# Top-32 attention with a squared-ReLU feed-forward: the end of the kernel rearranged

## The chip, the core and the metric

The kernel runs on one core of a Trainium2 chip. It is one program, launched once. The time is the device time of that launch in microseconds, the median of several runs. TensorE (PE) multiplies matrices, VectorE (DVE), ScalarE (ACT) and GpSimd (POOL) work elementwise, and SyncE (SP) issues nearly all DMAs. Each engine takes its instructions strictly in the order in which they were written down; semaphores tie the engines together.

## The reference

```python
B, H, S, D = 8, 8, 576, 64
scores = matmul(q, k.T) / sqrt(D)                      # (B, H, S, S)
kth    = 32nd largest of each row of scores
scores = where(scores >= kth, scores, -1e9)
attn   = exp(scores - max); attn = attn / (sum(attn) + 1e-9)
x = (attn @ v).transpose(0, 2, 1, 3).reshape(B*S, H*D) # (4608, 512)
h = x @ w_in                                           # (4608, 2048)
r = maximum(h, 0); g = r * r
out = g @ w_out                                        # (4608, 512), float32
```

Inputs and the output are float32. The attention scores are made in float32, attention weights times values and the feed-forward part in bfloat16.

## The kernel before

The attention rows are cut into 144 groups, numbered 0 to 143. A group is two blocks of 128 query rows (one for each of two heads) against all 576 keys. Each group goes through the same steps:

1. **Scores.** TensorE writes them into three PSUM banks (`ps<-qk`, L449). ScalarE copies them to one of six `s` buffers (`s<-ps`, L622).
2. **Top 32.** VectorE first takes the maximum of pairs and fours of columns (`ps<-ps,s` and `m<-ps,s` on L678, `f<-m,ps` on L688); POOL forms the other members of the pairs with integer sums and differences (L673). Then VectorE alternates "eight largest" (`c<-f`, L705) and "replace them" (`f<-c,f`, L709) three times, and a last "eight largest" over all 576 columns gives the 32nd value (`kth<-f`, L712). The cheap path assumes that the largest values are spread in a certain way over the columns.
3. **Flip.** ScalarE makes a penalty from `s` and `kth` (`w<-s,kth`, L720). TensorE transposes `s` and adds the steep penalty on top (`ps<-ident,s` on L452 and `ps<-steep_bf,w` on L449, nine blocks of 128 columns; the ninth uses the bank that the maxima of another group use). ScalarE takes the exponential (`p<-ps`, L754).
4. **Values.** TensorE multiplies with the values (`ps<-vb,p`, L449), ScalarE copies (`av<-ps`, L781), VectorE takes the reciprocal of the row sums (`rzall<-av`, L783), POOL scales (`x<-av,rzall`, L785), TensorE transposes (`ps<-ident_bf,x`, L452), ScalarE copies into a chunk of `xt` (L809).

When a chunk of rows has all its heads, it goes through the feed-forward part, in the function `feed`: TensorE multiplies with `win` (`ps<-xt,win`, L449), ScalarE takes the ReLU (`g<-ps`, L835), some engine squares it (`g<-g`; POOL on L849, ScalarE on L852, VectorE on L846), TensorE multiplies with `wo` (`ps<-wo,g`, L449), ScalarE copies the result (`o<-ps`, L869) and SP stores it (L877). The last two chunks have 128 rows each: 64 products `xt,win`, four squares of 128x512, and 16 products `wo,g` each. These products, the transposes of `x` and the value products share the two banks of the PSUM pool `psum`.

**Who sets the order.** Nothing is ordered by hand. Each step is declared with an engine, an assumed duration, a priority (a due time, smaller first), the tiles that it reads, writes and takes, and sometimes an extra delay. A list scheduler (`Plan.schedule`) then plays the program through on these assumed durations, and on each engine the ready step with the smallest priority goes next. The order that results is written out for each engine, with semaphore waits where needed. The constants shift due times: `TL` draws the attention steps after `kth` of the last 32 groups forward, `LAGL` delays the feed-forward steps of the chunks of the last batch (not the very last chunk), `LATE` delays the reciprocals, `SQ` chooses which squares go to POOL, `WC` is the due time of the weight casts. A change of a constant can so move instructions far from the place that it is about.

**The verdict.** The cheap top-32 is exact only for rows that meet its assumption. `verdict` checks this for all rows at once: VectorE compares the collected values and reduces them and `rzall` to three numbers per partition in `fone` (L978 to L986), TensorE sums them over the partitions with a product of one column (`ps<-fone`, L988), VectorE reduces the three sums to the integer `flag` (L990). Its steps have the priority 1e6, so they go last on their engines. Then every engine loads `flag` into a register and branches (L1022 to L1024): if it is above zero, the whole attention is done again with an exact program, `again`; with the inputs here it is zero and the branch skips that program. SP first waits until all stores of the main program have landed.

Of the kernel before, what the change touches and what calls it, by code (L numbers as in the profile page):

```python
# [291 lines left out]
def bass_top_k_attn__then__act_relu_squared_kernel(  # L292
# [31 lines left out]
    MQ = 19.61  # L324
    MP = 18.0
    MA = 18.27
    SQ = 5.15
    TA = 7.2
    TW = -0.14
    TL = 18.33  # L330
    WARM = 8
    WP = 6.49
    BW = 1
# [1 line left out]
    WEND = 70  # L335
    NL = 31.89
    WD = 3.33
    WC = 1.75
    WA = 1.13
    WN = 6  # L340
    NBO = 3.81
    LAG = 12.93
    STEP = 2.98
    LATE = 2.07
    LAGL = 17.86

    ident32 = sb("ident32", [P, P])
    ident_bf = sb("ident_bf", [P, P], BF16)
# [10 lines left out]
    fone = sb("fone", [P, 4])  # L359
# [31 lines left out]
    def tile(nm):  # L391
        return Tile(pools[nm])
# [4 lines left out]
    def bank(t, i=0):  # L397
        return ps32[:, BASE[t.pool.name] + t.slot + i, :]
# [8 lines left out]
    em = Emitter(nc)  # L407
    act, vec, gp, pe = nc.scalar, nc.vector, nc.gpsimd, nc.tensor
# [23 lines left out]
    CHUNKS = [[(0, 0, 128)], [(0, 128, 128)], [(0, 256, 256)]] if B0Q else [[(0, 0, 256)], [(0, 256, 256)]]  # L432
# [15 lines left out]
    def mm(o, l, r, start, stop=True):  # L448
        return pe.matmul(o, l, r, start=start, stop=stop, skip_group_check=True)  # L449
# [6 lines left out]
    def build(full, weights, pl):  # L456
# [358 lines left out]
        def feed(chunk, xt, tm, step):  # L815

            nt = sum(n_ for _, _, n_ in chunk)
            b = chunk[-1][0]
            last, end = b == NB - 1, chunk is CHUNKS[-1]
            kf = max(1, 512 // nt)  # L820
            lag = 0 if end else LAGL if last else LAG
            gs = [tile("g") for _ in range(NFB // kf)]
            for i, g in enumerate(gs):
                hh = Tile(psum)

                def fh(hh=hh, i=i):
                    for f in range(kf):
                        fb = kf * i + f
                        for ct in range(NCT):
                            ins = mm(bank(hh)[:, nt * f:nt * f + nt], win[:, ct, 128 * fb:128 * fb + 128],  # L830
                                     at(xt)[:, ct, 0:nt], ct == 0 and f == 0)
                    return ins

                def fr(hh=hh, g=g):
                    return act.activation(at(g)[:, 0:kf * nt], bank(hh)[:, 0:kf * nt], ACTF.Relu)  # L835

                tf = tm + step * i
                w_ = kf * nt
                ho = pl.op("pe", .03 + kf * 4 * (nt / 2340 + .002), tf + lag, fh, r=[xt], w=[hh], take=[hh, g],
                           after=weights if chunk not in FIRST else weights and weights[NCT * (kf * i // 8):][:NCT],  # L840
                           nbf=tf if not last else 0)
                if chunk in FIRST and weights:
                    first_h.append(ho)
                pl.op("act", .19 + w_ / 1200, tf + lag + .5, fr, r=[hh], w=[g])
                if end:
                    pl.op("dve", .1 + w_ / 1900, tf + lag + .8, lambda g=g: vec.tensor_tensor(  # L846
                        at(g)[:, 0:w_], at(g)[:, 0:w_], at(g)[:, 0:w_], ALU.mult), u=[g])
                elif last or i * SQ % 8 < SQ:
                    pl.op("gp", .15 + w_ / 480, tf + lag + 1, lambda g=g: gp.tensor_tensor(  # L849
                        at(g)[:, 0:w_], at(g)[:, 0:w_], at(g)[:, 0:w_], ALU.mult), u=[g])  # L850
                else:
                    pl.op("act", .19 + w_ / 1200, tf + lag + 1, lambda g=g: act.activation(  # L852
                        at(g)[:, 0:w_], at(g)[:, 0:w_], ACTF.Square), u=[g])
            for tb in range((nt + 127) // 128):
                n_ = min(128, nt - 128 * tb)
                op_, ob = Tile(psum), tile("o")
                to = tm + step * (len(gs) + 1 + 4 * tb)
                for sub in range(4):
                    def fo(sub=sub, op_=op_, tb=tb, n_=n_):
                        for fb in range(4 * sub, 4 * sub + 4):  # L860
                            c = nt * (fb % kf) + 128 * tb
                            ins = mm(bank(op_)[0:n_, :], at(gs[fb // kf])[:, c:c + n_], wo[:, fb, :], fb == 0)
                        return ins

                    pl.op("pe", .9, to + lag + step * sub, fo,
                          r=sorted({gs[fb // kf] for fb in range(4 * sub, 4 * sub + 4)}, key=lambda t: t.num),
                          w=[op_], take=[op_, ob] if sub == 0 else [], after=weights[8 + 2 * sub:10 + 2 * sub], order=[ho],
                          nbf=to + step * sub if not last else 0)
                pl.op("act", .6, to + lag + 4 * step, lambda op_=op_, ob=ob, n_=n_: act.copy(  # L869
                    at(ob)[0:n_, :], bank(op_)[0:n_, :]), r=[op_], w=[ob])  # L870
                rows, at_ = [], 0
                for b_, r0, m_ in chunk:
                    lo_, hi_ = max(at_, 128 * tb), min(at_ + m_, 128 * tb + n_)
                    if lo_ < hi_:
                        rows.append((lo_ - 128 * tb, hi_ - lo_, S * b_ + r0 + lo_ - at_))
                    at_ += m_
                pl.op("sp", 2.3, to + lag + 4 * step + 1, lambda ob=ob, rows=rows: [nc.sync.dma_start(  # L877
                    out[row:row + m_, :], at(ob)[p0:p0 + m_, :]) for p0, m_, row in rows],
                    r=[ob], ndma=len(rows), sem=lambda o: f"o{o.tiles[0].slot}")
# [13 lines left out]
        for b in range(NB):  # L893
# [3 lines left out]
            for hp, gi in seq:  # L897
# [6 lines left out]
                if state.get("more"):  # L904
                    state.pop("more")()
                tt = tg + PER + 2 - TA - TL * max(0, 1 - (NGRP - state["n"]) / NL)
                pt = attend(gi, st, wt, tt)
# [65 lines left out]
    def verdict(pl, kths, rzs):  # L973

        t = Tile(psum)
        G = NGRP
        fc = fcmp[:, :].rearrange("p (l g) -> p l g", l=2)
        x = pl.op("dve", .4, 1e6, lambda: vec.tensor_tensor(fc, c16[:, :, 0:G], c24[:, :, 0:G], ALU.min), after=kths)  # L978
        x = pl.op("dve", .4, 1e6, lambda: vec.tensor_tensor(fc, c8[:, :, 0:G], fc, ALU.min), after=[x])
        done = [pl.op("dve", .4, 1e6, lambda: vec.tensor_tensor(fc, kth[:, :, 0:G], fc, ALU.is_gt), after=[x])]  # L980
        d = pl.op("dve", .35, 1e6, lambda: vec.tensor_reduce(fone[:, 0:1], fcmp[:, :], AX.X, ALU.max), after=done)
        e = pl.op("dve", .35, 1e6, lambda: vec.tensor_reduce(fone[:, 1:2], rzall[:, :], AX.X, ALU.max), after=rzs)
        f = pl.op("dve", .35, 1e6, lambda: vec.tensor_reduce(fone[:, 2:3], rzall[:, :], AX.X, ALU.min), after=rzs)
        e = pl.op("dve", .1, 1e6, lambda: vec.tensor_scalar(
            fone[:, 1:2], fone[:, 1:2], 1e30, None, ALU.is_gt), after=[e])
        f = pl.op("dve", .1, 1e6, lambda: vec.tensor_scalar(  # L986
            fone[:, 2:3], fone[:, 2:3], 1e-30, None, ALU.is_lt), after=[f])
        g = pl.op("pe", .1, 1e6, lambda: pe.matmul(bank(t)[0:1, 0:3], fone[:, 3:4], fone[:, 0:3],  # L988
                                                   start=True, stop=True), w=[t], take=[t], after=[d, e, f])
        return pl.op("dve", .1, 1e6, lambda: vec.tensor_reduce(flag[:, :], bank(t)[0:1, 0:3], AX.X, ALU.max), r=[t])  # L990

    main = Plan()
# [19 lines left out]
    def stored(pl):  # L1012
        return {o.idx[0]: o.idx[1] for o in pl.order["sp"] if o.idx[0][1].startswith("o")}

    with nc.Block() as blk:
        def emit(e, eng):
            em.via(main, e)
            em.emit(main, e, eng)
            if e == "sp":
                for kk, vv in stored(main).items():  # L1020
                    eng.wait_ge(em.sem(kk), vv)
            eng.wait_ge(em.sems["dve"], flagged.idx[1])  # L1022
            val = eng.value_load(flag[0:1, 0:1], min_val=0, max_val=P)
            with eng.If(val > 0):  # L1024
                em.emit(again, e, eng)
                if e == "sp":
                    for kk, vv in stored(again).items():
                        eng.wait_ge(em.sem(kk), vv)

        @blk.gpsimd  # L1030
        def _(g_):
            emit("gp", g_)

        @blk.tensor
        def _(pe_):
            emit("pe", pe_)

        @blk.vector
        def _(v_):
            emit("dve", v_)  # L1040

        @blk.scalar
        def _(a_):
            emit("act", a_)

        @blk.sync
        def _(s_):
            emit("sp", s_)
# [28 lines left out]
```

## Time and profile before

| | |
|---|---|
| five runs | 869.27, 869.32, 870.0, 870.72, 875.24 us; median 870.0 |
| profiled execution | 869.82 us, its span 867.9 us, 22690 instructions |
| mean granted TensorE clock | 0.997 |
| last `kth` of VectorE (group 143) ends | 836.55 us |
| last product with `wo` on TensorE ends | 860.58 us |
| busy VectorE, TensorE, POOL, ScalarE | 824.1, 828.1, 788.1, 759.9 us |

The span runs from the first to the last instruction of the profiled execution; its own time is 1.9 us longer. Busy time counts computing instructions. Waits, loads of registers and branches are not counted; they appear under the line numbers of their source with the name of the engine's sequencer (SPq, PEldq and so on). L449 and L452 are helpers through which nearly all matrix products go, so these are told apart by their tiles.

### The profile page before, as it was taken

The numbers are of one execution on the slowest core, as the hardware profiler recorded it, in microseconds if no ns is written. First come the engines' busy times: TensorE is split into PE (matmuls) and PEld (weight loads), VectorE is DVE, ScalarE is ACT, GpSimd is POOL, SyncE is SP. The second block draws the span as 40 slices with busy tenths as digits, with TensorE's granted clock in tenths as the row PEclk, the third lists the DMA queues.
The fourth block names the chain that finished last, engine by engine and source line by source line (L and its number), as shares of the span: only waits on it lengthen the run. The fifth ranks groups of instructions, "written<-read, shape, count | busy, mean of one in ns | idle before, by whom it ended". The sixth has DMA issues, their size and how long they took to land.

```text
span 867.9 us, 22690 instructions
## 1 busy us (share of the span) xinstructions
PE 828.1 (95%) x8057; PEld 609.8 (70%) x8057; DVE 824.1 (95%) x3414; ACT 759.9 (88%) x1261; POOL 788.1 (91%) x826
## 2 busy tenths in 40 slices
PE   8898899999999999999999999999999999999996
PEld 3565677667776777767778677777778667687774
DVE  3899999999999999999999999999999999999970
ACT  3788999889998899989999799998989889898872
POOL 6798999999999989999999989999999988998961
PEclk9999999999999999999999999999999999999998
DMA  7583422111310223012120121301231021000001
GB/s 177 119 200 103 126 47 63 28 41 34 91 43 14 59 65 76 22 35 61 35 77 16 39 68 44 96 14 41 57 82 29 14 53 30 26 2 14 26 14 41
DMA packets 126985, 48.21 MB, mean 56 GB/s; under 512 B 119184, under 2 KB 119184, under 8 KB 126864
## 3 DMA queue, kind: packets, MB, share of 16 engines
q1 hardware_dynamic: 126192, 46.52, 21.4%
q8 instruction: 65, 1.06, 0.5%
q14 instruction: 56, 0.46, 0.2%
q10 hardware_dynamic: 672, 0.16, 0.1%
HBM read 37.22 MB, written 9.44 MB: 54 GB/s over the span
## 4 chain that ended last, share of the span: by engine, by line
DVE 70%; PE 17%; ACT 6%; issue 5%; POOL 1%; DVEq 0%; POOLq 0%
DVE f L709 22%; DVE c L705 18%; DVE kth L712 14%; PE ps L449 13%; DVE ps L678 5%; DVE f L688 5%; DVE m L678 5%; PE ps L452 4%; ACT p L754 2%; ACT s L622 1%; ACT w L720 1%; DVE rzall L783 1%; ACT g L835 1%; POOL f L673 0%; POOL t L673 0%
## 5 line engine op out<-in xcount | busy, mean ns | idle before, releaser
L709 DVE MATCH_REPLACE8 f<-c,f 128x104 f32<-128x104 f32 (+2 forms) x864 | 266.7, 314 | 0.0
L705 DVE MAX8 c<-f 128x8 f32<-128x104 f32 (+2 forms) x864 | 243.3, 318 | 0.1
L720 ACT ACTIVATE w<-s,kth 128x576 bf16<-128x576 f32 x288 | 223.2, 785 | 22.6 <-DVE kth L712 21.6
L452 PE MATMUL ps<-ident,s 128*128 128x128 f32 x1296 | 222.0, 280 | 9.2 <-ACT p L754 5.6
L673 POOL TENSOR_TENSOR t<-s 128x576 int32<-128x576 int32 x144 | 202.6, 1412 | 20.0 <-ACT s L622 19.9
L449 PE MATMUL ps<-qk 64*128 64x64 f32 (+3 forms) x1280 | 207.0, 442 | 2.9 <-DVE m L678 2.3
L712 DVE MAX8 kth<-f 128x8 f32<-128x576 f32 x288 | 207.9, 746 | 0.0
L673 POOL TENSOR_TENSOR f<-t,m 128x576 int32<-128x576 int32 x144 | 203.2, 1411 | 0.0
L449 PEld LDWEIGHTS ps<-qk 64*128 64x128 f32 (+1 forms) x1280 | 128.1, 176 | 77.4 <-issue 60.3
L622 ACT COPY s<-ps 128x1152 f32<-128x1152 f32 x144 | 161.3, 1120 | 22.8 <-PE ps L449 22.4
L754 ACT ACTIVATE p<-ps 128x1152 bf16<-128x1152 f32 x144 | 163.3, 1134 | 13.6 <-PE ps L449 12.6
L452 PEld LDWEIGHTS ps<-ident,s 128*128 128x128 f32 x1296 | 143.1, 141 | 34.2 <-ACT p L754 11.0
L449 PE MATMUL ps<-steep_bf,w 128*128 128x128 bf16 x1296 | 139.9, 219 | 0.0
L449 PE MATMUL ps<-wo,g 128*128 128x512 bf16 x576 | 139.7, 379 | 0.0
L673 POOL TENSOR_TENSOR t<-m 128x288 int32<-128x288 int32 x144 | 114.9, 798 | 18.8 <-ACT m L686 14.3
L449 PE MATMUL ps<-xt,win 128*128 128x256 bf16 (+1 forms) x1152 | 127.0, 261 | 4.1 <-ACT xt L809 2.3
L673 POOL TENSOR_TENSOR f<-t,f 128x288 int32<-128x288 int32 x144 | 114.9, 798 | 0.1
L449 PEld LDWEIGHTS ps<-xt,win 128*128 128x128 bf16 x1152 | 97.3, 98 | 19.7 <-ACT xt L809 3.7
L449 PEld LDWEIGHTS ps<-steep_bf,w 128*128 128x128 bf16 x1296 | 105.1, 100 | 4.0
L849 POOL TENSOR_TENSOR g<-g 128x512 bf16<-128x512 bf16 x92 | 95.5, 1042 | 7.6 <-ACT g L835 7.1
L835 ACT ACTIVATE g<-ps 128x512 bf16<-128x512 f32 x144 | 85.7, 606 | 5.7 <-PE ps L449 4.4
L449 PEld LDWEIGHTS ps<-wo,g 128*128 128x128 bf16 x576 | 51.8, 98 | 48.5 <-ACT g L835 0.5
(67 smaller groups left out, 909.9 us busy)
## 6 DMA issues: line engine op xcount, KB each, us to landing
rv<-in_v_dram SPq DMA_DIRECT2D x64, 128.0 KB, 2.4
out_dram<-o SPq DMA_DIRECT2D x32, 256.0 KB, 2.1
rk<-in_k_dram SPq DMA_DIRECT2D x63, 128.0 KB, 2.5
rq<-in_q_dram SPq DMA_DIRECT2D x62, 128.0 KB, 2.6
g<-in_moe_w_in_dram SPq DMA_DIRECT2D x8, 512.0 KB, 4.1
g<-in_moe_w_out_dram SPq DMA_DIRECT2D x8, 512.0 KB, 4.0
rv<-in_v_dram SPq DMA_DIRECT2D x96, 16.0 KB, 2.2
rq<-in_q_dram SPq DMA_DIRECT2D x32, 32.0 KB, 2.6
```

What stands on the lines that cost most here:

```text
L449: return pe.matmul(o, l, r, start=start, stop=stop, skip_group_check=True)
L452: return pe.matmul(o, i, ident, is_transpose=True, skip_group_check=True, **kw)
L622: cp = [pl.op("act", 1.2, tg - LEAD + 1, lambda: act.copy(at(st)[:, :, :], two(banks(ss), SECOND, S)), r=[ss], w=[st])]
L673: return pl.op("gp", dur, prio, lambda: gp.tensor_tensor(o().bitcast(I32), x().bitcast(I32), y().bitcast(I32), op), **kw)
L678: return vec.tensor_tensor(o, two(banks(ss)[:, a:], SECOND + HALF, QUART), two(at(st)[:, 0, HALF + a:], HALF, QUART), ALU.max)
L705: lambda i=i, t=t, c0=c0, c1=c1: vec.max(eighth(t, i), at(f)[:, i, c0:c1]),
L709: lambda i=i, t=t, c0=c0, c1=c1: vec.match_replace(at(f)[:, i, c0:c1], eighth(t, i), at(f)[:, i, c0:c1], NEG), hold=[f])]
L712: ks.append(chain(kth, i, prev[i] + [low], .665, lambda i=i: vec.max(eighth(kth, i), at(f)[:, i, :]), hold=[f]))
L720: pl.op("act", .77, tw + .8 * i, lambda i=i: act.activation(at(wt)[:, i, :], at(st)[:, i, :], ACTF.Relu, bias=kth[:, i, n:n + 1], scale=-1.0),
L754: pl.op("act", 1.15, tt + 1, lambda: act.activation(at(pt)[:, :, :].rearrange("p k q -> p (k q)"), banks(e)[:, 0:2 * S], ACTF.Exp, scale=0 ...
L835: return act.activation(at(g)[:, 0:kf * nt], bank(hh)[:, 0:kf * nt], ACTF.Relu)
L849: pl.op("gp", .15 + w_ / 480, tf + lag + 1, lambda g=g: gp.tensor_tensor(at(g)[:, 0:w_], at(g)[:, 0:w_], at(g)[:, 0:w_], ALU.mult), u=[g])
```

## The change

Three things are rewritten, and five constants have other values.

- SP reads the flag and branches like the other engines, without a wait before it. It waits for the stores of the main program after the branch, and, where the flag is above zero, inside the branch before it runs `again`.
- The product of the verdict (`ps<-fone`) has the priority 0 instead of 1e6.
- The squares of the last two chunks go to VectorE, not only those of the last one.

```diff
-    SQ = 5.15
+    SQ = 5.21
...
-    TL = 18.33
+    TL = 15.79
...
-    WC = 1.75
+    WC = 2.54
...
-    LATE = 2.07
+    LATE = 2.1
-    LAGL = 17.86
+    LAGL = 15.27
...
+            direct = chunk in CHUNKS[-2:]
...
-                if end:
+                if direct:
                     pl.op("dve", .1 + w_ / 1900, tf + lag + .8, lambda g=g: vec.tensor_tensor(
                         at(g)[:, 0:w_], at(g)[:, 0:w_], at(g)[:, 0:w_], ALU.mult), u=[g])
...
-        g = pl.op("pe", .1, 1e6, lambda: pe.matmul(bank(t)[0:1, 0:3], fone[:, 3:4], fone[:, 0:3],
+        g = pl.op("pe", .1, 0, lambda: pe.matmul(bank(t)[0:1, 0:3], fone[:, 3:4], fone[:, 0:3],
                                                    start=True, stop=True), w=[t], take=[t], after=[d, e, f])
...
             em.emit(main, e, eng)
-            if e == "sp":
-                for kk, vv in stored(main).items():
-                    eng.wait_ge(em.sem(kk), vv)
             eng.wait_ge(em.sems["dve"], flagged.idx[1])
             val = eng.value_load(flag[0:1, 0:1], min_val=0, max_val=P)
             with eng.If(val > 0):
+                if e == "sp":
+                    for kk, vv in stored(main).items():
+                        eng.wait_ge(em.sem(kk), vv)
                 em.emit(again, e, eng)
                 if e == "sp":
                     for kk, vv in stored(again).items():
                         eng.wait_ge(em.sem(kk), vv)
+            if e == "sp":
+                for kk, vv in stored(main).items():
+                    eng.wait_ge(em.sem(kk), vv)
```

## The prediction

> **What bounds the kernel now.** I read the page first (engine shares, chain that ended last), then busy time by stretches, then the timeline from the last top-k group to the end, then the instructions of the verdict's lines.
>
> ```profile
> PE 828.1 (95%) x8057; PEld 609.8 (70%) x8057; DVE 824.1 (95%) x3414; ACT 759.9 (88%) x1261; POOL 788.1 (91%) x826
> DVE 70%; PE 17%; ACT 6%; issue 5%; POOL 1%; DVEq 0%; POOLq 0%
> ...
> 100.00:650.00 550.00, 533.96 (x5231) 399.95 (x5227) 549.81 (x2288) 506.88 (x838) 526.29 (x531) 1.00 0.21 51
> 650.00:740.00 90.00, 88.37 (x883) 66.20 (x884) 89.92 (x376) 82.25 (x140) 82.44 (x84) 1.00 0.13 32
> 740.00:780.00 40.00, 39.93 (x413) 30.20 (x413) 39.92 (x167) 36.50 (x63) 37.89 (x41) 1.00 0.04 15
> 780.00:820.00 40.00, 39.28 (x398) 29.13 (x394) 40.00 (x170) 33.67 (x59) 37.08 (x41) 1.00 0.07 21
> 820.00:836.60 16.60, 16.09 (x212) 13.31 (x210) 16.57 (x71) 14.81 (x27) 13.85 (x17) 1.00 0.05 18
> 836.60:860.60 24.00, 22.62 (x260) 16.32 (x258) 5.64 (x15) 11.33 (x22) 7.90 (x10) 1.00 0.06 23
> 860.60:867.90 7.30, 0.10 (x2) 0.00 (x0) 0.15 (x1) 0.58 (x1) 0.00 (x0) 0.66 0.14 48
> ```
>
> The columns after the length are busy PE, PEld, DVE, ACT, POOL. From 100 to 836.6 us VectorE has no free time (0.4 us of 736.6). TensorE is nearly as full: from 650 to 860.6 it is idle for 1.63+0.07+0.72+0.51+1.38 = 4.3 us. So the kernel has three parts: VectorE's top-k until 836.6, TensorE's feed-forward remainder until 860.6, and 7.3 us in which hardly anything is computed.
>
> ```profile
> 848.14 12.46 PE ps L449 x128
> 860.59 0.02 issue
> 860.62 0.58 ACT o L869
> ...
> L1022 SPq EVENT_SEMAPHORE  x1: 1885/1885/1885, 861.6 to 861.6; - x1
> ...
> L1023 SPq TENSOR_LOAD <-flag x1: 468/468/468, 863.5 to 863.5; - x1
> L1023 SPq FUSED_REGOPS  x1: 183/183/183, 864.0 to 864.0; - x1
> ...
> L1024 ACTq COMPARE_BRANCH  x1: 58/58/58, 861.7 to 861.7; - x1
> L1024 PEldq COMPARE_BRANCH  x1: 4285/4285/4285, 861.8 to 861.8; - x1
> L1024 SPq COMPARE_BRANCH  x1: 45/45/45, 864.4 to 864.4; - x1
> ...
> L1015 PEldq DRAIN  x1: 73/73/73, 866.1 to 866.1; - x1
> L1015 SPq DRAIN  x1: 53/53/53, 867.7 to 867.7; - x1
> ```
>
> The end reads as a chain on SP: last store issued at about 861.2, a wait of 1.885 us for its landing, the load of the flag, register work, a branch at 864.4, and only 3.3 us later the drain with which every engine signs off. The others branched at 861.7 to 861.8 and drained by 866.1. SP is last by 1.5 us.
>
> **SP's branch ahead of the stores.** The wait for the last store moves behind load, register work and branch. SP's load then follows the last store's issue (861.6 instead of 863.5), so the branch comes at 862.4 and the drain, 3.3 us behind it, at 865.7. The store landed at about 863.5, inside those 3.3 us, so the moved wait costs nothing. Queued behind it is only SP's drain, for which all engines wait at the end. Gain 1.9 us. Two limits: PE drains at 866.1, but it waits for the flag today (load at 860.9, once the reduce on VectorE has ended); with the flag earlier its load follows its last matmul at about 860.4, so its drain comes near 865.6, just ahead of SP. If PE does not move, 1.5 us of gain remain. And SP's branch now falls among the others'; if it takes PE's 4.3 us from branch to drain instead of 3.3, 0.9 us remain. I take 1.9, since the three engines that branched together took 3.0 to 3.3.
>
> Advanced Engine Details and Errata (Control Flow Timing) of the Trainium skill gives about 108 ns for a compare-and-branch; SP's 45 ns row is below that, PE's 4285 ns far above. By that figure alone, as an estimate, overlapping the branch would bring 0.1 us plus load and register work, about 0.8 us in all; the rows with the 3.3 us behind the branch say 1.9. Runtime: NRT & Kernel Launch (Instruction fetch mechanics) of the Trainium skill says that a taken branch out of the fetched window stalls on a fetch, which is the kind of gap that these rows have.
>
> **The verdict's product earlier.** One product (two rows of 0.17 us on PE, issued together) and a 0.15 us reduce. Before, they stood behind PE's last matmul (860.51) and beside the 0.58 us copy of the last output, so off the path. Now the product stands in front of four `wo` products of the next-to-last chunk. It needs both reductions of `rzall` (0.45 and 0.44), which follow the last reciprocal: by the walk below 851.4 at the latest against 852 for PE, so no wait is expected; if it misses, PE waits under 1 us. It also takes one of the two banks of `psum` until the reduce, under the 0.86 us of those four products. Cost 0.1 us, bounds 0 and 1.
>
> **Squares of the next-to-last chunk.** Four POOL instructions of 1.04 us go, four VectorE ones come (L846: 577 ns once, 425 three times). VectorE is busy for 5.64 of the last 24.0 us, so the 1.7 to 2.3 us fit. In before the POOL squares ended at 851.96 and their `wo` products started at 853.51, with 64 `xt,win` products in between to hide them. In the new order these `wo` products follow the chunk's own `xt,win` directly, so the square is on PE's path, and 0.43 instead of 1.04 is what makes that order possible: worth nothing by itself.
>
> The 577 ns row is a square that began at 851.66 while POOL squared until 851.96: +0.15 us beside POOL. SBUF — State Buffer (SBUF: two separate sides) of the Trainium skill speaks against the move: a VectorE operation with two SBUF inputs and a GpSimd one that reads SBUF lock each other out for a whole instruction. By it, each of the four squares could wait for a POOL multiply (L785, 0.39): up to 1.6 us; by the row 0.6 us at most, mostly between matmuls.
>
> **The constants.** SQ 5.15 to 5.21 gives the same set of indices for `i*SQ % 8 < SQ`, and with WC 1.75 to 2.54 the start stays as it was: in the order of instructions TensorE, ScalarE, POOL and SP are equal in both kernels for the first half (PE's first difference is at about group 75 of 144), and VectorE differs by single swaps with a reciprocal. So the starved start (VectorE's waits of 3.1 us and less before 66 us) stays. From there the order shifts, at first to and fro, and from group 126 on with one sign, through TL and LAGL: up to the flip of group 135 TensorE has 10.2 us more feed-forward work in front of the same flip (80 `xt,win` of 0.056, 20 `wo` of 0.216, rest scores), up to the last one 3.5 us (16 `wo`). That work is only moved. VectorE's sum is unchanged, so its end stays at 836.6 unless it starves.
>
> What it does to TensorE's end I walk from the last scores. In before they end at 820.24; from there to 860.58 are 40.3 us, 1.9 of them idle (0.16+0.36+0.75+0.63), so 38.4 of work. In the new order 48 `xt,win` (2.7), 8 `wo` (1.7) and one flip block (0.2) stand ahead of the last scores instead: 33.8 us remain. But the last scores now stand behind a flip block that waits for VectorE's `f<-m,ps` of group 142: group 140 ends at 821.64, then in the new order two `c` (0.33), `f` (0.25), `ps` and `m` (0.72), a reciprocal (0.07), `f` (0.25), `f<-m,ps` (0.36): 823.6; plus 0.35 for the block and 1.3 for the scores: 825.3. End: 825.3 + 33.8 + idle. With 0.6 (one bank wait) to 1.9 (as before) it is 859.7 to 861.0; middle 860.4 against 860.58. Bounds: no idle at all since 650 us, -4.3; on the other side the rival below.
>
> **Sum.** Against the profiled execution, 869.82 us (span 867.9 and 1.9 around it; the median of the runs is 870.0, 0.2 higher): -1.9 (SP) -0.2 (TensorE) +0.1 (verdict) = 867.8.
>
> **Rivals.**
> *The order wins back TensorE's idle time* (0.19). The 4.3 us go in part: 2.3 or more gone gives 865.4 and less, all gone 863.5. For: the feed-forward work comes earlier, and the waits in front of the last flips (0.36, 0.75) are between instructions that change places. Against: TensorE still waits for reciprocals, which stand behind 2.4 us of verdict work on VectorE in both orders, now four instead of three.
> *Late flips starve VectorE* (0.14, of it 0.09 over 0.5%). There are six `s` buffers: the scores of group n+6 need the flip of n. In before, by the timeline, the flip ends 5 to 14.5 us after its `kth` (most at group 129), and VectorE has no wait. With the extra work in front it is 17 to 18 us for groups 127 to 136 (129: 14.5+3.5; 132: 10.8+7.0; 135: 7.0+10.2), 3 us beyond anything seen. The new order takes the pair maxima later, at about 4 groups (22.7 us) behind `kth` n; flip, scores (1.3) and copy (1.1) need some 20.5, so 2 us are left. It decides from a lateness of 4 us: 2 of cover and the 1.9 won. With 4 us of starvation 871.8, with 7 us 874.8, all of the 10.2 about 878.
> *The end does not shrink* (0.12): the wait was not the limit, because PE's branch (4.3 us) or a fetch beside the others sets the end. Then 0 to 0.9 is won: 868.8 to 869.7.
> *My forecast* (0.55): 866.2 to 868.8.
>
> **How the numbers follow.** About 0.5% (4.35 us) is what a measurement of this kernel tells from no change. Faster than 865.65 is most of the first rival and a little of the forecast's edge: 0.2. Slower than 874.35: 0.09. The rest 0.71. The range leaves out the deep ends of the first two rivals: 864.0 to 871.0.
>
> **What would show it.** Right: SP's flag load directly behind the last store's issue, its wait for the stores gone or some 17 ns, its drain 4.4 us after that load; other engines' flag loads before 860.9; VectorE's last `kth` within 1 us of 836.6; L449's last `wo` between 859 and 862; eight squares on VectorE of 0.43 to 0.58. Wrong: VectorE waits for `s` copies (`ps` from ACT) after 720 us, a `kth` end beyond 839, or a branch-to-drain gap on SP over 4 us.

## The result and the profile after

The changed kernel takes 867.32 us (median of 38 runs) against 869.23 us for the kernel before (66 runs beside it): ratio 0.9974, interval 0.9967 to 0.9982. That is 1.9 us, or 0.26%: clear of no change with this many runs, though less than the 0.5% that the prediction took as telling. Now and then an execution of either kernel loses some 6 us in its first 100 us (4 of those 66, and some in the groups below, whose intervals they widen); the first profiled execution of the changed kernel was one (873.16 us), so the lines below come from another execution of the same kernel (866.93 us, span 865.1).

In the changed file the load of the flag is L1021 (before L1023), the branch L1022, SP's wait for the stores L1032, the drain L1016, the verdict's product and its reduce L989 and L991, VectorE's squares L847, the ReLU L836, the last copy L870.

The page of the changed kernel, engine shares and the chain that ended last:

```profile
PE 823.2 (95%) x7994; PEld 608.6 (70%) x8057; DVE 825.3 (95%) x3418; ACT 761.7 (88%) x1261; POOL 783.6 (91%) x822
...
DVE 67%; PE 19%; ACT 6%; issue 5%; POOL 2%; DVEq 0%; POOLq 0%
```

VectorE has four instructions more, POOL four fewer: the moved squares. The record lost 63 products (7994 of 8057), so TensorE's busy time is too low here, and its waits are read from the view of waits instead. Busy time by stretches, cut at the end of the last `kth` (836.95) and of the last `wo` product (860.13):

```profile
100.00:650.00 550.00, 530.11 (x5181) 399.44 (x5223) 549.78 (x2286) 506.21 (x838) 526.24 (x532) 1.00 0.21 51
650.00:740.00 90.00, 87.77 (x881) 65.95 (x885) 90.00 (x377) 83.59 (x141) 81.29 (x82) 1.00 0.13 34
740.00:780.00 40.00, 39.22 (x382) 28.57 (x384) 39.41 (x166) 35.71 (x60) 37.24 (x40) 1.00 0.04 15
...
836.95:860.15 23.20, 22.35 (x245) 15.75 (x245) 7.03 (x21) 11.66 (x23) 2.07 (x5) 1.00 0.07 26
860.15:865.10 4.95, 0.00 (x0) 0.00 (x0) 0.00 (x0) 0.58 (x1) 0.00 (x0) 0.78 0.19 63
```

Three differences. The stretch after the last product is 4.95 us instead of 7.3. The one between the last `kth` and the last product is 23.2 instead of 24.0. And VectorE, full before, now lacks 0.59 us between 740 and 780, where it lacked 0.08. The view of waits gives most of that, for VectorE from 100 to 836 us (the same view of before has no line):

```profile
DVE ps L678 <- ACT s L622: 0.3, 1, 0.3
DVE ps L678 <- ACT p L754: 0.2, 1, 0.2
```

These are pair maxima that wait for a new `s` and for the PSUM bank that the exponential frees: VectorE starves by half a microsecond. The same two waits stand in all nine traces with the new constants and in none of the five with the old ones. Late flips explain them: the longer wait ends at 779.74 with the pair maxima of group 135, and the flip of group 129, whose `s` buffer that group takes, had ended only at 777.25, 18.3 us behind its `kth`; the scores of group 135 (to 778.5) and their copy (778.6 to 779.7) filled the 2.5 us between. The end, from the lines of the flag load, branch, SP's wait and drain (first and last start in us):

```profile
L1021 PEldq TENSOR_LOAD <-flag x1: 489/489/489, 857.8 to 857.8; - x1
L1021 SPq TENSOR_LOAD <-flag x1: 501/501/501, 861.2 to 861.2; - x1
...
L1022 PEldq COMPARE_BRANCH  x1: 3912/3912/3912, 858.7 to 858.7; - x1
L1022 SPq COMPARE_BRANCH  x1: 50/50/50, 862.0 to 862.0; - x1
...
L1032 SPq EVENT_SEMAPHORE  x1: 17/17/17, 864.6 to 864.6; - x1
...
L1016 PEldq DRAIN  x1: 73/73/73, 862.7 to 862.7; - x1
L1016 ACTq DRAIN  x1: 80/80/80, 864.4 to 864.4; - x1
L1016 SPq COMPARE_BRANCH  x1: 43/43/43, 864.7 to 864.7; - x1
L1016 SPq DRAIN  x1: 13/13/13, 864.9 to 864.9; - x1
```

SP issues the last store at 860.8, loads the flag at 861.2, branches at 862.0, and needs 2.6 us until its next instruction; the wait there takes 17 ns. SP's drain still comes last, now only 0.5 us behind ScalarE's. PE loads the flag at 857.8, 2.3 us before its last product ends.

### The profile page after: what moved, and what is told of

It is laid out like the page before. It is cut to its first block, busy times and chain, and to the rows that moved or that the text cites. A ratio compares the mean times of both kernels' runs of the same rounds, so it can differ in the third digit from the quotient of the medians.

```text
span 871.3 us, 22671 instructions
## 1 busy us (share of the span) xinstructions
PE 833.8 (96%) x8057; PEld 610.7 (70%) x8057; DVE 825.2 (95%) x3418; ACT 762.3 (87%) x1261; POOL 783.8 (90%) x822
## 4 chain that ended last, share of the span: by engine, by line
DVE 67%; PE 19%; ACT 6%; issue 5%; POOL 1%; DVEq 0%; POOLq 0%
DVE f L709 21%; DVE c L705 17%; PE ps L449 15%; DVE kth L712 14%; DVE ps L678 5%; DVE f L688 5%; DVE m L678 5%; PE ps L452 5%; ACT p L754 2%; ACT s L622 1%; ACT w L720 1%; ACT g L836 1%; DVE rzall L783 1%; POOL t L673 0%; ACT qk L579 0%
## 5 line engine op out<-in xcount | busy, mean ns | idle before, releaser
L449 PE MATMUL ps<-qk 64*128 64x64 f32 (+3 forms) x1280 | 209.3, 445 | 2.7 <-DVE m L678 2.1
L449 PEld LDWEIGHTS ps<-xt,win 128*128 128x128 bf16 x1152 | 96.9, 98 | 18.4 <-ACT xt L809 2.7
L850 POOL TENSOR_TENSOR g<-g 128x512 bf16<-128x512 bf16 x88 | 91.6, 1044 | 4.9 <-ACT g L836 3.8
L836 ACT ACTIVATE g<-ps 128x512 bf16<-128x512 f32 x144 | 86.2, 606 | 6.1 <-PE ps L449 4.8
```

## The experiments

Every time is a median of a dozen runs, or of the number given; "before" is the kernel before on the same chip: 869.38 us in the first group (up to the constants alone), 869.44 in the second (up to the old constants), 869.25 in the third (the product alone and the last three). Where two groups are compared, the distances from their own "before" are what counts. An interval reaches about 1 us or more to either side, so steps of a few tenths rest on the traces.

**The changed kernel again.** No edit.

> The changed kernel again, since its first profiled execution was 6 us longer than its usual runs and lost them before 100 us. My theory (SP's branch gives 1.9 us, TensorE's end hardly moves): 867.2 us, last kth at 836 to 837.5 us, last wo between 859.5 and 861, SP's drain about 4.4 us after its flag load. Rival (TensorE's idle time was won back, SP gave little): last wo before 859, and SP's drain less than 1 us earlier behind the last store than before.

Measured: 867.18 us, ratio 0.997 (0.9958 to 0.9982). The lines above are from this run.

**SP's part alone**, on the kernel before; **SP's wait back in front**, in the changed kernel (the same edit the other way). The cut leaves out the wait inside the skipped branch, which is as in the change.

```diff
             em.emit(main, e, eng)
-            if e == "sp":
-                for kk, vv in stored(main).items():
-                    eng.wait_ge(em.sem(kk), vv)
...
+            if e == "sp":
+                for kk, vv in stored(main).items():
+                    eng.wait_ge(em.sem(kk), vv)
```

> The kernel before, with SP's wait behind the branch alone. My theory: 1.9 us faster than before, ratio 0.9978; the order of all other work is that of before, so the last wo stays at 860.6. But PE's flag load still comes at 860.9 there, and PE drained at 866.1: then 1.5 to 1.6 us, ratio 0.9982. Rival (the end does not shrink, since PE's branch or the fetch sets it): 0 to 0.9 us, ratio 0.999 to 1.0.

> The changed kernel with SP's wait in front of the branch again; everything else as in the changed kernel. My theory: 1.9 us slower than the changed kernel, so 0.2 to 0.4 us faster than before (ratio 0.9995). Rival (the gain comes from TensorE's order): still 2 us faster than before, ratio 0.9975.

Measured: alone 868.43 us, ratio 0.9985 (0.9973 to 0.9997), a gain of 0.95; taken back out of the changed kernel 869.21, ratio 0.9995 (0.9982 to 1.0007), a loss of 2.03 against the changed kernel. By the medians the same edit is worth twice as much in the changed kernel. The drains of the changed kernel with the wait back, then branches and drains of the kernel with SP's part alone, show why:

```profile
L1016 PEldq DRAIN  x1: 73/73/73, 863.1 to 863.1; - x1
L1016 ACTq DRAIN  x1: 80/80/80, 864.7 to 864.7; - x1
L1016 SPq DRAIN  x1: 53/53/53, 867.1 to 867.1; - x1
```

```profile
L1021 PEldq COMPARE_BRANCH  x1: 4593/4593/4593, 861.6 to 861.6; - x1
...
L1021 SPq COMPARE_BRANCH  x1: 50/50/50, 862.3 to 862.3; - x1
...
L1015 SPq DRAIN  x1: 13/13/13, 865.6 to 865.6; - x1
L1015 PEldq DRAIN  x1: 73/73/73, 866.2 to 866.2; - x1
```

In the changed kernel with the wait back, SP drains 2.4 us behind ScalarE, the next to last, so its part can give all of its 2 us. With SP's part alone SP is early as planned, but the flag is known only at 860.7, and PE's 4.6 us of branch then end last. What follows: on the kernel before, SP's wait was the limit by about 1 us; behind it stood PE's branch, and the product at priority 0 is what takes that away (shown below).

**The constants alone**, on the kernel before (`SQ`, `TL`, `WC`, `LATE`, `LAGL` as in the change).

> The kernel before with the five constants alone: verdict's product last, squares of the next-to-last chunk on POOL, SP waits first. My theory: TensorE's work is only moved; 0 to 1 us slower than before (ratio 1.000 to 1.001), the squares on POOL now in TensorE's path. Rival (order wins back idle time): 1 us or more faster. Rival (late flips starve VectorE): VectorE waits for s copies after 720 us and the time is 2 us or more longer.

Measured: 869.32 us, ratio 0.9994 (0.9982 to 1.0007): nothing. Last `kth` to last `wo` is 23.66 us instead of 24.03, but VectorE starves by the same 0.3 and 0.2 us as in the changed kernel. A gain of 0.36 and a loss of 0.5 of that kind would about cancel; the times can't show either by itself.

**SP's part and the product**, on the kernel before; **the product back at 1e6**, in the changed kernel; later **the product alone**, on the kernel before. SP's edit as above, and

```diff
-        g = pl.op("pe", .1, 1e6, lambda: pe.matmul(bank(t)[0:1, 0:3], fone[:, 3:4], fone[:, 0:3],
+        g = pl.op("pe", .1, 0, lambda: pe.matmul(bank(t)[0:1, 0:3], fone[:, 3:4], fone[:, 0:3],
```

> The kernel before with SP's wait behind the branch and the verdict's product at priority 0 (TensorE then has it 128 xt,win and wo products earlier); constants and squares of before. SP's part alone gave about 1.0 us, with PE's drain as the last of all (866.2, SP 865.6). Theory (PE's branch was what cut SP's gain): PE reads the flag while its last products still run, drains before 864, SP is last again; 1.8 to 2.1 us faster than before, ratio 0.9978, so 0.7 to 1.0 faster than SP's part alone. Rival (the product costs TensorE a bank or a wait): no faster than SP's part alone, ratio 0.9985 or above, last wo after 860.8.

> The changed kernel with the verdict's product at priority 1e6 again, so behind the last wo. Theory: all engines read the flag at 860.5 or later and PE's 4.3 to 4.6 us from branch to drain set the end: 0.8 to 1.2 us slower than the changed kernel, ratio to before 0.9983 to 0.9987. Rival (product's place is worth nothing): equal to the changed kernel, 0.9975.

> The kernel before with one edit, the verdict's product at priority 0; SP still waits for the stores first. Theory (the product's gain comes only through PE's branch, which ends last when SP's wait is out of the way): here SP ends last by 1.5 us whatever PE does, so nothing is won and the product costs TensorE up to 0.2 us: 869.4 to 869.7 us, ratio 1.000 to 1.0005, PE's drain near 861 to 862 and SP's near 867.7. Rival (the product's place is worth 0.4 to 0.7 us by itself, since an early flag helps every engine): 868.7 to 869.0 us.

Measured: both parts 867.78 us, ratio 0.9974 (0.9958 to 0.9989). Product taken back 867.61, ratio 0.9974 (0.9958 to 0.999); there PE loads the flag at 860.0, its branch takes 4573 ns and it drains last:

```profile
L1016 SPq DRAIN  x1: 13/13/13, 865.0 to 865.0; - x1
L1016 PEldq DRAIN  x1: 8/8/8, 865.6 to 865.6; - x1
```

So by the medians the product adds 0.65 us to SP's part (868.43 to 867.78) and 0.4 us in the changed kernel (867.61 to 867.18). These compare two groups and the intervals overlap; that PE's branch ends last without the product, and 2 us and more before SP with it, is what shows the cause.

The product alone is the surprise: 870.42 us (11 runs), ratio 1.0014 (1.0005 to 1.0023), 1.2 us *slower*. Neither the theory (nothing) nor the rival (faster) had it. SP's own waits in that kernel, from 850 us on (in before: 1.9):

```profile
SPq L1022 <- DMA out_dram<-o: 3.8, 1, 3.8
```

The last store lands 1.9 us later after its issue. (This trace is of the slowest of the eleven runs, 871.75 us; the median lost 1.2, so 1.9 is more than the usual delay.) Transfers around it, first before (40 slices over 861.6 to 864.6, the store issued at 861.2), then the product alone (862.2 to 866.0, issued at 861.8). The first line is the busy share in tenths, the second GB/s:

```profile
DMA  0000007999999793603000009000000000000000
GB/s 0 0 0 0 0 0 273 355 410 410 410 382 410 300 382 137 246 0 109 0 0 0 0 0 218 0 0 0 0 0 0 0 0 0 0 0 0 0 0 0
...
q8 instruction: 1, 0.02, 2.5%
```

```profile
DMA  0000099998983020000000001010010000000020
GB/s 0 0 0 0 22 345 366 517 345 345 366 323 108 22 86 0 0 0 0 0 0 0 0 0 22 0 22 0 0 22 22 22 22 22 22 0 0 0 86 0
...
q8 instruction: 1, 0.02, 2.8%
```

In before the store's data has passed by 862.9, and the one packet of queue q8, 16 KB of instructions, comes behind it, at 863.4 (the single 9). With the product alone most of the store has passed by 863.6, and then a thin rest follows at 864.5 to 865.6: 22 GB/s in slices of 95 ns, one packet of 2 KB at a time. The transfer records put the packet of q8 at 862.91, among the store's data, for 1674 ns; the first late packet of the store starts at 864.57, just as it ends. The store is 128 packets of 2 KB and 16 of 4 bytes; the late rest is eight and one of them, a sixteenth, which is what one of the 16 DMA engines would carry.

The 14 kept traces bear this out. In each, the first of two q8 packets starts 1.0 to 1.6 us after the start of PE's branch and the second 3.2 to 4.2 us later; other 8 KB packets of instructions come on queue q14. In eight traces such a packet of either queue falls among the last store's data, and the last packet of the store then ends 2.3 to 3.7 us after the store's issue; in the six others, where none comes before the last 0.1 us of the data, 1.7 to 1.8. In four of the eight (the product alone, both parts, the old constants below, and the changed kernel itself, there behind a q14 packet) exactly eight 2 KB packets are left when the instruction packet ends, and the first of them starts within 0.02 us.

So an earlier flag can let PE's branch fetch its code just when the store goes out, and a share of the store queues behind the code. Whether the two meet is a matter of tenths: in the changed kernel with SP's wait back, the flag is early too, but the q8 packets (860.33, 863.73) miss the store's data (862.2 to 863.2). With SP's wait in front, SP pays for a meeting; behind the branch it does not: with both parts the packet (862.04) also falls on the store, which lands 3.4 us after issue, inside SP's branch.

Runtime: NRT & Kernel Launch (Instruction fetch mechanics) of the Trainium skill says that a sequencer fetches code by a DMA queue of its own in blocks of 16 KiB, and that a taken branch out of the fetched window waits for such a fetch. The 16 KB packets beside PE's 3.5 to 4.6 us agree; that such a block delays other transfers is shown by these runs alone.

**The next-to-last chunk's squares back on POOL**, and **the old constants back**, both in the changed kernel.

```diff
-                if direct:
+                if end:
```

> The changed kernel with the squares of the next-to-last chunk on POOL again. With the constants alone TensorE waited 0.86 us in front of that chunk's wo products. Theory (prediction: the quick square is what makes the new order possible): that wait returns, last wo 0.3 to 0.6 us later than in the changed kernel against the last kth, time 0.3 to 0.6 us longer, ratio 0.9978 to 0.9982. Rival (squares worth nothing): 0.9975.

> The changed kernel with the five constants of before: SP's branch first, early product, squares on VectorE, but TensorE's order at the end as in before. Theory (constants move work and gain nothing): equal to the changed kernel within 0.4 us, ratio 0.9972 to 0.998. Rival (constants win back idle time of TensorE): 1 us or more slower than the changed kernel, 0.9985 or above.

Measured: without the squares 867.88 us, ratio 0.9987 (0.9965 to 1.0009); with the old constants 867.9, ratio 0.9973 (0.995 to 0.9997). Each costs about 0.7 us by the medians, intervals overlapping. TensorE's waits from 836 to 862 us, first without the squares, then with the old constants, then in the changed kernel:

```profile
PE ps L449 <- ACT g L835: 0.9, 2, 0.6
PE ps L452 <- POOL x L785: 0.5, 1, 0.5
```

```profile
PE ps L452 <- ACT g L836: 0.8, 1, 0.8
PE ps L452 <- DVE flag L991: 0.2, 1, 0.2
```

```profile
PE ps L452 <- POOL x L785: 0.4, 1, 0.4
PE ps L452 <- ACT g L836: 0.3, 1, 0.3
```

Last `kth` to last `wo` is 23.89, 24.02 and 23.18 us. This distance settles what the times leave open, since it repeats: 23.18 or 23.19 in all four traces of TensorE's order in the changed kernel. With the old constants the squares on VectorE gain nothing (24.02 against 24.03 in before), and the new constants without them gain 0.14: neither shortens TensorE's end by itself as both do together (0.85).

**SP's branch ahead of the last store**, **reciprocals ahead of the verdict**, and **both**, in the changed kernel. The first splits SP's list; in short:

```diff
-            em.emit(main, e, eng)
+            late = main.order["sp"][-1:] if e == "sp" else []
+            em.emit(main, e, eng, [o for o in main.order[e] if o not in late])
...
             with eng.If(val > 0):
                 if e == "sp":
+                    em.emit(main, e, eng, late)
...
+                with eng.If(val < 1):
+                    em.emit(main, e, eng, late)
```

The second changes `after` of the verdict's first step on VectorE:

```diff
-ALU.min), after=kths)
+ALU.min), after=kths + rzs)
```

> The changed kernel with one edit: SP reads the flag and branches before it issues the last store, which it then issues behind the branch. Theory (what is left of SP's end is load, register work, and 2.7 us from the branch to its next instruction, all behind the last store's issue): the load moves from 861.2 to about 859.5, where VectorE's flag is known, so the branch's 2.7 us lie beside the last product and the copy of the last output. The store goes out about 1.0 us later than before or at the same time, if the branch is through by then, and its landing, 1.9 us after issue, is then last: SP's drain near 863.1 to 863.8, and ScalarE's drain (864.4 in the changed kernel) becomes the last. Gain 0.4 to 0.6 us against the changed kernel, 866.6 to 866.9. Rival (every taken branch costs SP the same 2.7 us, and this form has two): the store comes out late or the second branch follows it, and the kernel is 0 to 2 us slower than the changed one.

> The changed kernel with one edit: the verdict's first step on VectorE waits for the last reciprocals, so these go ahead of some 2.2 us of verdict work. Theory (TensorE loses 0.45 us at 840 to a transpose of x whose reciprocal stands behind verdict work): that wait goes, the last product with wo ends about 22.8 us after the last kth instead of 23.2, and the kernel is 0.3 to 0.5 us faster than the changed one, 866.7 to 866.9. Rival (another wait, for a bank or a ReLU, is just behind it): 23.2 stays and the time is that of the changed kernel.

> The changed kernel with both edits, SP's branch ahead of the last store and the reciprocals ahead of the verdict work. If they are independent: 0.7 to 1.1 us faster than the changed kernel, 866.1 to 866.5, ratio to the kernel before about 0.9962. Rival: the first edit leaves ScalarE's branch as the end, which follows the flag and not the last product; then the reciprocals, which move the last product but may delay the flag, add nothing: the time of the first edit alone.

Measured: branch ahead of the store 866.4 us (6 runs, the slowest 867.04), ratio 0.9967 (0.9955 to 0.9979). SP loads the flag at 854.2, not at 859.5 as expected: the flag is known at 852.4. The drains are as expected, ScalarE's last:

```profile
L1016 SPq DRAIN  x1: 13/13/13, 863.8 to 863.8; - x1
L1016 ACTq DRAIN  x1: 80/80/80, 864.4 to 864.4; - x1
```

Reciprocals first: 867.0 us (9 runs), ratio 0.9971 (0.9961 to 0.9981), hardly a gain. The wait at 840 went and the last product came 22.88 us behind the last `kth`, as expected, but the chain has a new piece at 853.6:

```profile
853.07 0.42 DVE g L847
853.49 0.09 DVE flag L991
853.58 0.05 issue
853.62 6.32 PE ps L449 x64
```

The flag is later, its reduce stands behind a square, and TensorE waits 0.24 us for the bank that it holds. In that execution SP also took 3.4 us from branch to next instruction instead of 2.6, and ScalarE 0.8 us more from branch to drain; why is open.

Both: 866.23 us, ratio 0.997 (0.9957 to 0.9983). By the medians this beats both kernels, by 3.0 us the one before and by some 0.8 the changed one at the same distance from its before; the intervals of ratios overlap, so the last step is an indication. How much of it the reciprocals bring is not settled (866.4 to 866.23).

## Why the prediction was right, and where it was not

**The sum** was -2.0 from 869.82; measured -1.9 from 869.23. The absolute 867.8 is 0.5 us above 867.32, nearly all of it from the starting point: the profiled execution lay 0.6 us above the long-run median, and the median of the five runs 0.8. That the sum came out so closely is in part luck: SP's term was right for the reason given, but the rest, -0.1 forecast and -0.17 measured, holds a gain of 0.85 us that was not forecast in that size and a later end of VectorE that was not forecast at all.

**SP's branch ahead of the stores: -1.9 predicted, -2.03 measured** inside the changed kernel. The load stands directly behind the store's issue, the wait is 17 ns, as predicted. From branch to next instruction SP took 2.6 us, not 3.3; the store landed 3.2 us after issue, not 2.3, and still inside that cover, with 0.6 us to spare. SP's drain came 3.7 us after its load; the sign of "4.4 us" did not even follow from the prediction's own times (861.6 to 865.7 is 4.1). The step that failed is the one on PE: "with the flag earlier its load follows its last matmul at about 860.4, so its drain comes near 865.6". PE's load came at 857.8, 2.3 us before its last product ended at 860.13, and the drain at 862.7: PE's sequencer was past products that still had to run, so its branch ran beside them. The limit given for "PE does not move", 1.5 us, was the right mechanism and too generous: with the product at 1e6 the gain on the kernel before was 0.95. PE's branch took 4.59 us there instead of 4.29, and the 1.5 was read from an execution 0.6 us above the long-run median.

**The verdict's product: +0.1 predicted.** Its cost on TensorE is about that: last `kth` to last `wo` is 23.18 us with it and 22.96 without, 0.2; in TensorE's order of before it costs nothing (24.02 or 24.03 in all five traces). Its worth had been booked under SP's part and not named as a condition. By itself it is +1.2, with SP's part -0.65 or -0.4. "Cost 0.1, bounds 0 and 1" missed that its flag decides when PE fetches code, which can delay the last store.

**Squares: "worth nothing by itself", "what makes that order possible".** Right: nothing with the old constants, 0.7 us by the medians and by the distance (23.89 to 23.18) with the new ones. All of VectorE's squares in the changed kernel took 416 to 427 ns; POOL had 2.07 us of work left in the last 23, so the question whether the two engines hinder each other was hardly put to the test.

**The constants: -0.2 predicted** for TensorE's end, at 860.4. The walk held: last scores at 825.06 (predicted 825.3), last `wo` at 860.13 (859.7 to 861.0). What it lacked is a pair that works against each other: TensorE's end relative to the last `kth` shrank by 0.85 us (24.03 to 23.18), and VectorE lost 0.5 us in waits. Its last `kth` comes at 836.4 to 837.2 us in the five traces with the old constants and at 836.7 to 837.5 in seven of usual length with the new ones, 0.3 later in the mean and within the spread. "VectorE's sum is unchanged, so its end stays at 836.6 unless it starves": it starved, a little. The flips stood 17.2 to 18.4 us behind `kth` for groups 127 to 136 (by the start of their last product), as worked out. The "2 us left" of cover were not there: VectorE was to take the pair maxima "about 4 groups (22.7 us)" behind `kth`, but it took those of group 135 at 20.8 us behind the `kth` of group 129, and would have taken them at 20.5. Everything in the change but SP's part sums to -0.17 (869.38 to 869.21, no change by the interval), where -0.1 was predicted.

**The rivals.** *Late flips starve VectorE* was there in its smallest form, 0.5 us. *The order wins back TensorE's idle time* too: 0.85 of the 4.3 us. *The end does not shrink, because PE's branch sets it* is what SP's part alone would have met; the product at priority 0 kept it away.

## What to carry to other kernels

At the end of a program, list for each engine when its last branch can start and when it drains, and move all of them: taking the last one away brings only the distance to the next. A wait that moves behind a long gap (here SP's 2.5 to 3.4 us behind its branch) is covered by it, also for a transfer that takes somewhat longer than usual. Judge parts of a change in the company that they will have: here one part alone gave 0.95 us, one lost 1.2, and together they gave 1.7. Where times differ by tenths, look for a distance inside the trace that repeats to hundredths.

## What was not expected of the hardware

- PE's branch takes 3.5 to 4.6 us in its own record, the others' 45 to 72 ns, with 2.5 to 3.4 us from SP's branch to its next instruction.
- PE's sequencer loads the flag and branches up to 4.0 us before PE's last product ends (857.2 against 861.2, with the product alone).
- A 16 KB packet of instructions among a store's packets went with a landing of a 256 KB store 4.2 us after its issue instead of 2.3, a sixteenth of the store starting only when that packet had ended.
